# Two layers of SSM convolution and SiLU layer, forward and backward: half of the first layer's activations stored turned, and where the w2 gradient's matmuls are woven in

## The chip, the core and the metric

The kernel runs on one core of a Trainium2 chip. The metric is device microseconds of one execution, lower is better. The core has five engines that are named here as the profile does: PE (TensorE, matmuls; its weight loads are PEld), DVE (VectorE), ACT (ScalarE), POOL (GpSimd) and SP (SyncE, which only issues DMAs here). "SPq" is SP's queue of DMA issues. Each engine works through its own instructions in order and waits on semaphores for the others.

## The reference

Sequence length S = 2048, width D = 448, hidden width F = 1792, batch 1, bfloat16. Four residual blocks are applied to one input, and the kernel returns the output and the gradients with respect to all inputs but `B_x`, for a given `grad_out`:

```python
def _fwd_reference(A_q, A_k, A_v, A_shift_k, A_ssm_k, A_ssm_D, B_x, B_w1, B_w2):
    # _A_ref: k is convolved with a 4-tap kernel and multiplied by v (kv);
    #         y = irfft(rfft(kv, 2S) * rfft(ssm_k, 2S))[:S] + kv * ssm_D;  returns q * y
    # _B_ref: silu(x @ w1) @ w2
    x = A_q
    x = x + _A_ref(_layernorm(x), A_k, A_v, A_shift_k, A_ssm_k, A_ssm_D)
    x = x + _B_ref(_layernorm(x), B_w1, B_w2)
    x = x + _A_ref(_layernorm(x), A_k, A_v, A_shift_k, A_ssm_k, A_ssm_D)
    x = x + _B_ref(_layernorm(x), B_w1, B_w2)
    return x

def reference(...):
    _out, _vjp = jax.vjp(_f, A_q, A_k, A_v, A_shift_k, A_ssm_k, A_ssm_D, B_w1, B_w2)
    return (_out, *_vjp(grad_out))
```

What matters for this case are the gradients of the weights. With a0, a1 the SiLU activations (S x F) of the two dense layers, and g0, g1 the gradients that arrive at those layers' outputs (g1 is `grad_out`), the gradient of w2 is a0ᵀ·g0 + a1ᵀ·g1. The gradient of w1 is built the same way from the layers' normalised inputs and the gradients before the SiLU.

## The kernel before

**Stages.** `_ssm_prefix` computes the convolution y of kv once with a Fourier transform that is written as matmuls; y serves both layers. `Main.run` then goes over the sequence in four chunks of 512 rows, three times: forward of the first dense layer (in the code `L == 0`; the change's short title calls it layer 1), then forward and backward of the second layer (`L == 1`), then backward of the first. `_ssm_suffix` transforms the gradient of y back (a first transform step per index n2, `_fft_stage1`, sixteen of them; transposes; a spectrum and an inverse in seven pieces; two last inverse transforms) and computes the gradients of k, v, the filters and D.

**Activations.** `Main.h` computes half of the hidden width (seven of the fourteen strips of 128) of one chunk: matmuls, SiLU into `aT` on ACT, a copy of the input into `dT` (on DVE, partly ACT) for the slope. Both are feature-major: partition = feature, free = position. `aT` and `dT` have three buffers each. For the first layer `dT` goes to DRAM (`DT_d`, L640) and `aT` too (`store_plain`, L507, `AP_d`); after the first chunk each half also loads one piece of the turned weights (`next_piece`, L516, transposing DMAs). The matmuls of the weight gradients need position on the partitions, so `AP_d` is read back with a transposing DMA. For the second layer `store_turned` (L503/L504) is used: two transposing DMAs from SBUF to SBUF into the single buffer `turned`, and a plain store into `A_d` that is kept back (`self.late`) until the next `flush`; it is read back with a plain DMA.

**Woven matmuls.** The w2 gradient (`_gw2`) goes over fourteen strips `ft`; a strip has two jobs (`_job`), one for each layer: one load of 512 KB into a buffer `dstat` (L896 transposed, L898 plain), then 16 matmuls (L900) with X (g0) or GO (g1) as the moving operand, all 32 into one PSUM tile; then a copy `dout` on ACT and a store. `_gw1` does the same for w1 with `mov` (the normalised inputs, loaded from DRAM: N_d3 at L1032 and N_d1 at L922) and `GH_d`, `GP_d`; there each strip's `dout` also gets a memset on POOL (L959) and a transposing DMA (L936). In all there are 28 strips, 896 matmuls. They are generators: `fill(n)` and `weave(n)` take the next n matmuls and put them at this place of PE's order, with whatever loads and stores they bring. `fill` is used in the backward of the first layer: in `ga` (the product with w2ᵀ, seven PSUM tiles per chunk, 1 each and 2 for the first; none in the first chunk) and in `gn` (the product with w1ᵀ and the sums of the layer norm's backward in `ln_bwd`, four tiles of 128 rows per chunk, 2 each). `weave` is used in the suffix, where `_in_turn` holds PE to the order of the program: 4 after each of the sixteen first transform steps, 16 around each of the transposes, 2 to 5 in the spectrum and the inverse, 3 and 10 in the next stage, 4 and then 34 for each of the eight last transform steps, and at the end all that are left.

**Order.** The order on the engines is the program's, as a scheduler places it when the kernel is built; `issue_after` and `keep_in_program_order` are constraints on it. All loads and nearly all stores stand in SP's one queue.

**The end.** The gradient of k (`grad_k`, eight pieces of two positions each, multiplications and additions on DVE and a store at L1123) is computed for pieces 0 to 5 inside the last transform loop and for 6 and 7 after the last `weave`. Its buffers `gkv` are shared with `gsk`, the gradient of the shift kernel, whose two stores are issued by POOL (L1181, L1182).

Of the kernel before, what the change touches and what calls it, by code (L numbers as in the profile page):

```python
# [11 lines left out]
BF16 = mybir.dt.bfloat16  # L12
# [5 lines left out]
P = 128  # L18
S = 2048
# [3 lines left out]
NT = 16  # L23
DC = 112
ND = 4
NF = 14
# [93 lines left out]
@with_exitstack  # L120
def kernel(
    ctx: ExitStack,
    tc: tile.TileContext,
    A_q: bass.AP,
    A_k: bass.AP,
    A_v: bass.AP,
    A_shift_k: bass.AP,
    A_ssm_k: bass.AP,
    A_ssm_D: bass.AP,
    B_x: bass.AP,  # L130
    B_w1: bass.AP,
    B_w2: bass.AP,
    grad_out: bass.AP,
    out_0: bass.AP,
    out_1: bass.AP,
    out_2: bass.AP,
    out_3: bass.AP,
    out_4: bass.AP,
    out_5: bass.AP,
    out_6: bass.AP,  # L140
    out_7: bass.AP,
    out_8: bass.AP,
):
    nc = tc.nc
    k = K()
    k.tc, k.nc = tc, nc
    k.bal = _Bal(nc)
    for nm, v in (("A_q", A_q), ("A_k", A_k), ("A_v", A_v), ("A_shift_k", A_shift_k), ("A_ssm_k", A_ssm_k),
                  ("A_ssm_D", A_ssm_D), ("B_w1", B_w1), ("B_w2", B_w2), ("grad_out", grad_out)):
        setattr(k, nm, v)  # L150
    k.outs = [out_0, out_1, out_2, out_3, out_4, out_5, out_6, out_7, out_8]
    C = make_fft_consts()

    dram = ctx.enter_context(tc.tile_pool(name="dram", bufs=1, space=DRAM))
    k.KS_d = dram.tile([S, D], BF16, name="KS_d")
    k.SPEC_d = {nm: dram.tile([128, SPEC], BF16, name=f"spec_{nm}") for nm in ("K", "KV")}
    k.N_d = [dram.tile([S, D], BF16, name=f"N_d{i}") for i in range(4)]
    k.DT_d = dram.tile([4, 2, P, NF // 2, 512], BF16, name="DT_d")
    k.A_d = dram.tile([P, NF, NT, P], BF16, name="A_d")
    k.AP_d = dram.tile([NF, P, S], BF16, name="AP_d")  # L160
    k.GH_d = dram.tile([P, NF, NT, P], BF16, name="GH_d")
    k.GP_d = dram.tile([NF, P, S], BF16, name="GP_d")

    bf = mybir.dt.np(BF16)
    m1b = np.ascontiguousarray(C["M1"], dtype=np.float32).astype(bf)
    minv = (np.transpose(m1b.astype(np.float32), (3, 1, 2, 0)) * np.float32(C["inv_scale"])).astype(bf)
    k.m1_h = nc.inline_tensor(np.ascontiguousarray(m1b.reshape(P, -1)), name="c_m1")
    gs_h = nc.inline_tensor(np.ascontiguousarray(C["Gs"].reshape(P, -1)).astype(np.float32).astype(bf), name="c_gs")
    k.minv_h = nc.inline_tensor(np.ascontiguousarray(minv.reshape(P, -1)), name="c_minv")

    keep = ctx.enter_context(tc.tile_pool(name="keep", bufs=1))
    k.ident = keep.tile([P, P], BF16, name="ident")
    make_identity(nc, k.ident[:])
    k.gs_h = gs_h
    k.rstd = [keep.tile([P, J], FP32, name=f"rstd{i}") for i in range(4)]
    k.warm = keep.tile([P, 4], FP32, name="warm")
    k.mhalf = keep.tile([P, 4], FP32, name="mhalf")
    nc.gpsimd.memset(k.mhalf[:], -0.5)
    nc.scalar.activation(k.warm[:], k.mhalf[:], ACT.Silu)
    k.wk = ctx.enter_context(tc.tile_pool(name="wk", bufs=1))  # L180
    k.dp = ctx.enter_context(tc.tile_pool(name="dp", bufs=1))
    k.yk = ctx.enter_context(tc.tile_pool(name="yk", bufs=1, side="right", reuse_waits="tile"))
    k.Ysb = k.yk.tile([P, J, D], BF16, name="Ysb", tag="Y")
    _ssm_prefix(k)
    k.w1sb = k.wk.tile([P, ND, F], BF16, name="w1sb", tag="WA")
    nc.sync.dma_start(out=k.w1sb[:, 0:3, :], in_=k.B_w1[0:384].rearrange("(c p) f -> p c f", p=P))
    nc.sync.dma_start(out=k.w1sb[:, 3, :], in_=k.B_w1[320:448])
    k.w2sb = k.wk.tile([P, NF, D], BF16, name="w2sb", tag="WB")
    nc.sync.dma_start(out=k.w2sb[:], in_=k.B_w2.rearrange("(c p) d -> p c d", p=P))
    k.psum = ctx.enter_context(tc.tile_pool(name="psum", bufs=1, space=PSUM, reuse_waits="tile"))  # L190
    k.xg = ctx.enter_context(tc.tile_pool(name="xg", bufs=1, side="right", reuse_waits="tile"))
    k.Xp = k.xg.tile([P, NT, 512], BF16, name="X", tag="X")
    k.X = k.Xp[:, :, :D]
    k.gYb = k.xg.tile([P, NT, D], BF16, name="gYb", tag="GY")
    k.bal.reset()
    with ExitStack() as es:
        m = Main(k, es)
        m.run()
    _ssm_suffix(k)


# [51 lines left out]
def _pm(ap2d):  # L253
    return ap2d.rearrange("(p j) d -> p j d", j=J)
# [225 lines left out]
class Main:  # L480
# [136 lines left out]
    def h(self, c, L, nT, half, hold, pre=None):  # L617
        nc, k = self.nc, self.k
        aT = self.td.tile([P, NF // 2, 512], BF16, name="aT", tag="T", bufs=3)
        dT = self.td.tile([P, NF // 2, 512], BF16, name="dT", tag="D", bufs=3)  # L620
        hold.append((aT, dT))
        d0 = pre() if pre else None
        for ft0, n, at in ((0, 2, 1), (2, 2, 0), (4, 2, 1), (6, 1, 1)) if half == 0 else ((7, 1, 1), (8, 2, 1), (10, 2, 0), (12, 2, 1)):
            ps = k.psum.tile([P, 2, 512], FP32, name="ps_h", tag="mm", bufs=2)
            self.contract(ps, self.w1sb, nT, ft0, n, at)
            o = ft0 - 7 * half
            a = aT[:, o:o + n, :]
            tm = dT[:, o:o + n, :]
            last = nc.scalar.activation(a, ps[:, 0:n, :], ACT.Silu)  # L629
            e = nc.scalar if o == 4 or (o, c, L, half) == (0, 0, 0, 0) else nc.vector  # L630
            _copy(nc, e, tm, ps[:, 0:n, :])
            k.bal.add("act", 0.52 * n)
            k.bal.add(*(("act", 0.52 * n) if e is nc.scalar else ("dve", 0.6 * n)))
        if L == 1:
            if half == 1:
                with self.tc.issue_after(last.ins):
                    for _, d in hold:
                        self.slope(d)
        else:
            nc.sync.dma_start(out=k.DT_d[c, half], in_=dT[:])  # L640
            self.store_plain(nc.sync, k.AP_d, aT, c, half)
            if c > 0:
                self.next_piece()
        if L == 1:
            self.store_turned(k.A_d, aT, c, half)
        return d0

    def out(self, c, aT, last):
# [77 lines left out]
    def gn(self, c, L, ghT, nb, gres, na, hook=None):  # L726
        nc, k = self.nc, self.k
# [4 lines left out]
        for tl in range(4):  # L732
# [6 lines left out]
            k.bal.add("act", 0.75)  # L739
            k.pe_engine = mm.ins.engine  # L740
            if L == 0:
                self.fill(2)
            if hook:
                hook(tl, mm.ins, last_u.ins)
            g1 = G[:, tl, :]
# [36 lines left out]
    def run(self):  # L782
        k, nc = self.k, self.nc
# [28 lines left out]
        for c in range(4):  # L812
# [26 lines left out]
            na, nb = na1, nb1  # L839
            if c < 3:  # L840
                gb = gb_next
        k.jobs = _gw2(k, k.dp, range(2), [(k.dp, "dstat", 3)], first=k.go_jobs.ins)
        bb = nc.cur_bb.bb

        def fill(n):
# [58 lines left out]
def _gw2(k, pool, fts, slots, bufs=2, first=None):  # L904
    nc = k.nc
    for ft in fts:
        ps = k.psum.tile([P, 512], FP32, name="ps_d", tag="tr", bufs=2)
        for L, mov in ((0, k.X), (1, k.GO)):
            slot = slots.pop(0)
            slots.append(slot)  # L910
            yield from _job(k, ps, k.A_d if L else k.AP_d, ft, mov, slot, L == 0, L == 1, first, L == 0)
        o = pool.tile([P, D], BF16, name="dout", tag="dout", bufs=bufs)
        nc.scalar.copy(o[:], ps[:, :D])
        nc.sync.dma_start(out=k.outs[8][ft * P:(ft + 1) * P, :], in_=o[:])
# [50 lines left out]
def _ssm_suffix(k):  # L965
    nc, tc, bal = k.nc, k.tc, k.bal
# [6 lines left out]
    with ExitStack() as es:  # L973
# [4 lines left out]
        both = [(k.dp, "dstat", 3), (k.dp, "dstat", 3), (dp2, "dstat", 2), (k.dp, "dstat", 3), (dp2, "dstat", 2)]  # L978

        def jobs():  # L980
            yield from k.jobs
            yield from _gw2(k, k.dp, range(2, NF), both)
            yield from _gw1(k, dp2, both)

        jobs = jobs()

        def weave(n):
            with _in_turn(k):
                for _ in zip(range(n), jobs):
                    pass  # L990
# [4 lines left out]
        Z = sp.tile([P, NDH, P], BF16, name="Zg")  # L995
        ksf = k.yk.tile([P, J, D], BF16, name="ksf", tag="Y")
        B1k = A1[:].rearrange("p a c n s -> p (a c n s)").rearrange("p (q d) -> p q d", d=D)
        for n2 in range(16):
            with _in_turn(k):
                _fft_stage1(k, n2, k.gYb[:, n2, :], A1, psum, nc.scalar if n2 < 12 else None)  # L1000
            weave(4)
# [106 lines left out]
        def grad_k(g):  # L1108
            acc = p2.tile([P, 2, D], FP32, name="gk_acc", tag="gK", bufs=4)
            gk = p2.tile([P, 2, D], BF16, name="gk", tag="gk", bufs=2)  # L1110
            last = None
            for j in range(4):
# [7 lines left out]
                    last = acc  # L1120
                else:
                    last = pj
            nc.sync.dma_start(out=out2_pm[:, 2 * g:2 * g + 2, :], in_=gk[:])  # L1123

        out3_pm = _pm(k.outs[3][0])
        out2_pm = _pm(k.outs[2][0])
# [89 lines left out]
```

## Time and profile before

| | |
|---|---|
| time, median of 3 runs | 748.47 us (746.36 to 749.24) |
| the profiled execution | 746.53 us, its span 744.4 us |
| PE busy | 690.7 us, 93% of the span |
| DVE, ACT, POOL busy | 507.0, 424.3, 61.6 us |
| mean granted TensorE clock | 0.985 |
| DMA moved | 172.77 MB, 232 GB/s over the span |

The span runs from the first to the last instruction of the profiled execution; the time contains some 2 us around it. The stages in it: the prefix to about 95 us, the first layer's forward to about 205, the second layer to about 410 (its last part overlaps the next), the first layer's backward to 516, the suffix to the end.

From the groups of instructions and the DMA issues, for the parts that the change touches:

| what | count | duration |
|---|---|---|
| L900 matmul of a woven job (128x448) | 896 | 352 ns recorded, pipelined |
| L736 matmul of `gn` (128x448) | 448 | 353 ns recorded, pipelined |
| AP_d<-aT, plain store from the forward, 896 KB | 8 | 4.1 us to landing |
| turned<-aT, transposing, SBUF to SBUF | 16 | 4.3 us to landing |
| A_d<-turned, plain store, 896 KB | 8 | 4.0 us to landing |
| out_dram<-gk, 224 KB | 8 | 2.7 us to landing |

Matmuls are pipelined, so a recorded duration is longer than the distance from one to the next.

### The profile page before, as it was taken

The page shows a single profiled execution, that of the slowest core. Times are in us where ns is not written, and L with a number is a line of the kernel's source. Part 1 is how long each engine was busy: PE and PEld are TensorE (multiplying, and loading weights), DVE is VectorE, ACT ScalarE, POOL GpSimd, SP SyncE. Part 2 cuts the span into 40 slices and gives each one's busy share as a digit, 9 for nine tenths or more (in the row PEclk, how much of TensorE's full clock was granted, in tenths as well). Part 3 has the DMA queues.
Part 4 walks back from the last instruction along what each step waited for, and adds up shares of the span by engine and source line. Part 5 has one row for each costly group of instructions (what it writes and reads, how often), then busy time and mean ns, then how long its engine had stood idle before and what let it go on. Part 6 is the DMA issues. An engine that isn't in the chain of part 4 may idle for free.

```text
span 744.4 us, 12143 instructions
## 1 busy us (share of the span) xinstructions
PE 690.7 (93%) x4724; PEld 363.0 (49%) x4753; DVE 507.0 (68%) x1059; ACT 424.3 (57%) x539; POOL 61.6 (8%) x109
## 2 busy tenths in 40 slices
PE   5988789999999998999999999994999999999996
PEld 5766533444344443444443444442556677555553
DVE  4878878787733597895949979786117773498241
ACT  4688767767437578487576577644525766321001
POOL 1144221111100002000000000000000000000000
PEclk9999989999999999999999999997999999999999
DMA  9959948999575878879999986964998997999797
GB/s 306 238 182 274 358 176 289 274 250 247 163 152 143 204 162 206 184 204 203 223 235 275 362 232 184 312 160 120 292 216 216 327 302 276 320 242 262 163 214 137
DMA packets 232869, 172.77 MB, mean 232 GB/s; under 512 B 178890, under 2 KB 215566, under 8 KB 231660
## 3 DMA queue, kind: packets, MB, share of 16 engines
q1 hardware_dynamic: 226446, 149.46, 76.8%
q0 software_dynamic: 5744, 22.19, 8.8%
q8 instruction: 37, 0.61, 0.3%
q10 hardware_dynamic: 622, 0.35, 0.2%
q14 instruction: 20, 0.16, 0.1%
HBM read 62.24 MB, written 63.77 MB: 169 GB/s over the span
## 4 chain that ended last, share of the span: by engine, by line
PE 46%; DVE 27%; ACT 8%; issue 7%; DMA 7%; POOL 2%; another core or an unknown queue 2%; SPq 1%; DVEq 0%; ACTq 0%; POOLq 0%
PE ps_d L900 17%; PE ps_h L537 6%; PE ps_o L654 5%; PE ps_g L537 4%; PE ps_n L736 4%; DVE lb_junk L711 4%; DMA KB<-Z 3%; DVE dT L113 3%; DVE lb_u L722 3%; DVE lb_u L754 2%; DVE X L723 2%; PE ps_v L232 2%; PE ps_v L233 2%; DMA K_sb<-in_A_ssm_k_dram 2%
## 5 line engine op out<-in xcount | busy, mean ns | idle before, releaser
L900 PEld LDWEIGHTS <-dstat 128*128 128x128 bf16 x896 | 85.4, 98 | 80.7 <-issue 4.7
L537 PE MATMUL ps_h<-nT,w1sb 128*128 128x512 bf16 (+1 forms) x432 | 103.2, 388 | 7.7 <-DVE dT L113 5.1
L537 PE MATMUL ps_g<-gT,w2T 128*128 128x512 bf16 (+1 forms) x448 | 96.0, 381 | 3.9 <-ACT ghp L686 3.9
L736 PE MATMUL ps_n<-w1T,ghT 128*128 128x448 bf16 x448 | 90.2, 353 | 2.2 <-DVE ghT L694 2.0
L629 ACT ACTIVATE aT<-ps_h 128x1024 bf16<-128x1024 f32 (+1 forms) x64 | 58.4, 915 | 57.6 <-PE ps_h L537 40.6
L654 PE MATMUL ps_o<-w2sb,aT 128*128 128x448 bf16 x448 | 90.1, 353 | 0.0
L900 PE MATMUL ps_d<-mov,dstat 128*128 128x448 bf16 x448 | 87.7, 352 | 2.4 <-DMA dstat<-GP_d 2.3
L113 DVE CAST dT<-ps_h 128x1024 bf16<-128x1024 f32 (+1 forms) x55 | 58.3, 1063 | 30.1 <-ACT aT L629 30.1
L537 PEld LDWEIGHTS <-w1sb 128*128 128x128 bf16 (+1 forms) x448 | 36.3, 97 | 71.5 <-issue 43.7
L537 PEld LDWEIGHTS <-w2T 128*128 128x128 bf16 (+1 forms) x448 | 35.3, 96 | 62.8 <-issue 30.2
L736 PEld LDWEIGHTS <-ghT 128*128 128x128 bf16 x448 | 42.8, 98 | 44.2 <-DVE ghT L694 4.3
L686 ACT CAST ghp<-ps_g 128x1024 bf16<-128x1024 f32 x56 | 55.3, 1006 | 15.1 <-PE ps_g L537 11.2
L654 PEld LDWEIGHTS <-aT 128*128 128x128 bf16 x448 | 42.4, 98 | 42.5 <-issue 3.9
L900 PE MATMUL ps_d<-X,dstat 128*128 128x448 bf16 x224 | 54.6, 360 | 0.2
L900 PE MATMUL ps_d<-GO,dstat 128*128 128x448 bf16 x224 | 51.7, 353 | 0.2
L960 ACT CAST dout<-ps_d 128x448 bf16<-128x448 f32 x14 | 7.5, 534 | 65.4 <-PE ps_d L900 37.3
L738 ACT ACTIVATE lb_u<-ps_n,rstd 128x448 f32<-128x448 f32 x32 | 20.3, 633 | 40.4 <-DVE X L723 17.7
L233 PEld LDWEIGHTS <-pb 128*128 128x128 bf16 x336 | 32.5, 98 | 9.0 <-DVE pb L452 5.6
L232 PEld LDWEIGHTS <-pa 128*128 128x128 bf16 x336 | 32.8, 98 | 7.2 <-DVE pa L451 4.3
L694 DVE TENSOR_TENSOR ghT<-dT,ghp 128x1024 bf16<-128x1024 bf16 (+1 forms) x32 | 19.7, 619 | 20.4 <-ACT ghp L686 20.3
L614 ACT ACTIVATE dTl<-dTl 128x1024 bf16<-128x1024 bf16 (+1 forms) x32 | 29.8, 944 | 4.8 <-DMA dTl<-DT_d 4.8
L655 DVE TENSOR_TENSOR X<-X,ps_o 128x448 bf16<-128x448 bf16 x32 | 19.7, 615 | 16.3 <-PE ps_o L654 16.2
(187 smaller groups left out, 1089.6 us busy)
## 6 DMA issues: line engine op xcount, KB each, us to landing
DT_d<-dT SPq DMA_DIRECT2D x8, 896.0 KB, 6.3
AP_d<-aT SPq DMA_DIRECT2D x8, 896.0 KB, 4.1
A_d<-turned SPq DMA_DIRECT2D x8, 896.0 KB, 4.0
GH_d<-turned SPq DMA_DIRECT2D x8, 896.0 KB, 4.5
dTl<-DT_d SPq DMA_DIRECT2D x8, 896.0 KB, 7.6
dstat<-A_d SPq DMA_DIRECT2D x14, 512.0 KB, 4.5
GP_d<-ghT SPq DMA_DIRECT2D x8, 896.0 KB, 9.6
dstat<-GH_d SPq DMA_DIRECT2D x14, 512.0 KB, 4.2
```

The source lines that it names most:

```text
L113: eng.tensor_copy(out, in_)
L232: nc.tensor.matmul(o, lhsT=pa[:, i * P:(i + 1) * P], rhs=k.Gsb[:, ga, :], start=True, stop=False)
L233: nc.tensor.matmul(o, lhsT=pb[:, i * P:(i + 1) * P], rhs=k.Gsb[:, gb, :], start=False, stop=True)
L537: self.nc.tensor.matmul(o, lhsT=w[lo:hi, b, f:f + P], rhs=r, start=(seen[u] == 1), stop=(seen[u] == ND))
L614: self.k.last_slope = self.nc.scalar.activation(s, s, ACT.Derivative_silu)
L629: last = nc.scalar.activation(a, ps[:, 0:n, :], ACT.Silu)
L654: nc.tensor.matmul(po[:, :D], lhsT=aT[ft // 7][0][:, ft % 7, tl * P:(tl + 1) * P], rhs=self.w2sb[:, ft, :], start=(ft == 0), stop=(ft == N ...
L686: k.last_gh = nc.scalar.copy(gh[:], ps[:])
L711: nc.vector.scalar_tensor_tensor(out=junk[:], in0=u0, scalar=1.0, in1=n_t, op0=ALU.mult, op1=ALU.mult, accum_out=cp[:, 1:2])
L722: nc.vector.scalar_tensor_tensor(out=u0, in0=n_t, scalar=cc[:, 1:2], in1=u0, op0=ALU.mult, op1=ALU.add)
L736: mm = nc.tensor.matmul(pn[:, :D], lhsT=ghT[ft // 7][:, ft % 7, tl * P:(tl + 1) * P], rhs=self.w1T[:, ft, :], start=(ft == 0), stop=(ft == ...
L900: i = k.nc.tensor.matmul(ps[:, :D], lhsT=st[:, t, :], rhs=mov[:, t, :], start=start and t == 0, stop=stop and t == NT - 1)
```

## The change

Four things are edited. In the forward of the first layer the first half of the hidden width (strips 0 to 6) goes through `store_turned` into its own DRAM tensor, ahead of the store of `dT`; the second half is stored plain as before, ahead of the store of `dT`, and after a `flush` that issues the kept-back store of the turned half. Accordingly strips 0 to 6 of the first layer are read back with plain loads and strips 7 to 13 with transposing ones, as before. In the last chunk of the first layer's backward, `gn` takes 12 woven matmuls per tile in the place of 2, from three strips in the place of two. In front of the suffix's first transform step 16 more are woven in. The last two stores of the gradient of k are issued by POOL in the place of SP.

```diff
-    k.A_d = dram.tile([P, NF, NT, P], BF16, name="A_d")
-    k.AP_d = dram.tile([NF, P, S], BF16, name="AP_d")
+    k.A_d = [dram.tile([P, n, NT, P], BF16, name=f"A_d{n}") for n in (NF // 2, NF)]
+    k.AP_d = dram.tile([NF // 2, P, S], BF16, name="AP_d")
...
         else:
+            if half == 0:
+                self.store_turned(k.A_d[0], aT, c, 0)
+            else:
+                self.flush()
+                self.store_plain(nc.sync, k.AP_d, aT, c, 0)
             nc.sync.dma_start(out=k.DT_d[c, half], in_=dT[:])
-            self.store_plain(nc.sync, k.AP_d, aT, c, half)
             if c > 0:
                 self.next_piece()
         if L == 1:
-            self.store_turned(k.A_d, aT, c, half)
+            self.store_turned(k.A_d[1], aT, c, half)
...
             if L == 0:
-                self.fill(2)
+                self.fill(2 if c < 3 else 12)
...
-        k.jobs = _gw2(k, k.dp, range(2), [(k.dp, "dstat", 3)], first=k.go_jobs.ins)
+        k.jobs = _gw2(k, k.dp, range(3), [(k.dp, "dstat", 3)], first=k.go_jobs.ins)
...
-            yield from _job(k, ps, k.A_d if L else k.AP_d, ft, mov, slot, L == 0, L == 1, first, L == 0)
+            plain = L == 0 and ft >= NF // 2
+            yield from _job(k, ps, k.AP_d if plain else k.A_d[L], ft - plain * (NF // 2), mov, slot, L == 0, L == 1, first, plain)
...
-            yield from _gw2(k, k.dp, range(2, NF), both)
+            yield from _gw2(k, k.dp, range(3, NF), both)
...
         B1k = A1[:].rearrange("p a c n s -> p (a c n s)").rearrange("p (q d) -> p q d", d=D)
+        weave(NT)
         for n2 in range(16):
...
-            nc.sync.dma_start(out=out2_pm[:, 2 * g:2 * g + 2, :], in_=gk[:])
+            (nc.sync if g < 6 else nc.gpsimd).dma_start(out=out2_pm[:, 2 * g:2 * g + 2, :], in_=gk[:])
```

## The prediction

> **What bounds the kernel now.** I read the busy shares first, then the table of busy time by stretch, then the order of time on each engine inside the one stretch that stood out, and last the end of the kernel. TensorE is busy 690.7 of 744.4 us, so it is the bound almost everywhere, and the question is where its 53.7 idle us lie. The table by stretches of 20 us (columns: length, then busy us and count of PE, PEld, DVE, ACT, POOL, then granted clock, DMA share, GB/s) answers it for the second half:
>
> ```profile
> 480.00:500.00 20.00, 20.00 (x99) 8.47 (x98) 17.19 (x47) 11.56 (x17) 0.79 (x3) 1.00 0.64 155
> 500.00:520.00 20.00, 10.08 (x46) 4.79 (x45) 15.06 (x47) 7.41 (x12) 0.54 (x1) 0.77 0.58 132
> 520.00:540.00 20.00, 20.00 (x115) 10.69 (x114) 3.06 (x3) 10.83 (x13) 0.00 (x0) 0.97 0.89 274
> 540.00:560.00 20.00, 20.00 (x141) 11.60 (x140) 1.57 (x2) 5.13 (x5) 0.00 (x0) 1.00 1.05 223
> ```
>
> From 480 us until about 720 us PE is full, but for one hole of 9.9 us, at half clock when it ends. What ends the hole is in the order of time on PE and on ACT:
>
> ```profile
> 506.25 0.92 PE L900 MATMUL ps_d<-GO,dstat 128*128 128x448 bf16 x4
> 517.09 0.91 PE L210 MATMUL ps_s<-gYb,M1s 128*128 128x448 bf16 x2 [9.92 <-ACT A1g L111]
> 517.79 1.70 PE L900 MATMUL ps_d<-X,dstat 128*128 128x448 bf16 x4
> ```
> ```profile
> 515.49 0.76 ACT L716 ACTIVATE lb_v<-na_l,lb_cc 128x448 bf16<-128x448 bf16 x1 [4.26 <-DVE lb_cc L713]
> 516.16 1.69 ACT L111 CAST A1g<-ps_s 128x896 bf16<-128x896 f32 x2
> ```
>
> The suffix's transform has two PSUM buffers. PE fills both by 506 us. Their evictions to A1g stand on ACT behind lb_v of the last tile, which waits for the DVE sums of the last chunk; those run without a gap (about 4.74 us per tile) until 515.1. So PE has no work while DVE finishes. The same groups of four matmuls take 0.92 us before the hole and 1.70 after it.
>
> The end of the kernel, in the order of time of the last 55 us, PE, SP, POOL and DVE:
>
> ```profile
> 712.22 0.15 POOL L959 MEMSET dout<- 128x64 bf16 x1 [8.31 <-DMA do<-dout]
> 712.90 0.63 POOL L1181 DMA_DIRECT2D out_dram<-gsk  x1 [0.53 <-issue]
> 717.49 0.63 DVE L1117 TENSOR_TENSOR gkp<-gks,skb 128x896 bf16<-128x896 bf16 x1 [13.01 <-DMA out_dram<-gsk]
> 727.20 1.09 DVE L1119 TENSOR_TENSOR gk<-gk_acc,gkp 128x896 bf16<-128x896 f32 x1
> 728.32 0.46 SPq L1123 DMA_DIRECT2D out_dram<-gk  x1
> 728.89 0.37 SPq L898 DMA_DIRECT2D dstat<-GH_d  x1
> 729.61 5.00 PE L900 MATMUL ps_d<-mov,dstat 128*128 128x448 bf16 x24 [2.09 <-DMA dstat<-GP_d]
> 732.92 1.25 PEld L900 LDWEIGHTS <-dstat 128*128 128x128 bf16 x8 [0.55 <-DMA dstat<-GH_d]
> ```
>
> The last two stores of gk are in SP's queue ahead of the last loads of dstat. SP waits there for DVE, and PE then waits for the loads. DVE itself starts that work at 717.5, because its buffer is held by gsk, whose store stands on POOL behind a memset.
>
> **What the Trainium skill says.** "TensorE: Matmul & The Clock Gate", section "What's actually happening": a PE idle for a window of about 3.4 us falls to half clock and needs about 3.4 us of work to regain it. The trace agrees: the granted clock is 0.50 from 511 to 520 us, 1.00 from 523. "Advanced Engine Details and Errata", section "X-Bar Transpose (TRN2)": transposing DMAs are about as fast as ordinary ones. The trace agrees only roughly: the transposed dstat<-AP_d takes a median of 5.9 us to land, the plain dstat<-A_d 4.5, and SP's issue of the first a median of 3.1 us against 0.35. "DMA: Bandwidth & Descriptors", section "Issuing engines are not separate DMA queues": another issuing engine saves only sequencer time. That is all that moving two gk stores to POOL can do, and it is what is short at 728 us.
>
> **The change part by part.** One woven matmul costs 0.189 us (16 of them in 3.03 us in the chain of waits).
>
> 1. *More fill.* Up to the transform, the kernel before issues 8 + 16 + 16 + 16 = 56 woven matmuls (2 a tile in the last step of a chunk, 8 in its first). The new one issues 8 + 16 + 16 + 8 + 48 = 96, which are exactly the three w2 strips of 32, and then 16 more ahead of the transform: 112. So 56 x 0.189 = 10.6 us of PE work move to the front of the transform, out of the last stretch (174 matmuls after the last special product before, 118 now).
>
> 2. *Does the hole take them?* The last chunk's sums start on PE at 492.6. A tile is now 14 + 12 matmuls, 2.65 + 2.27 = 4.92 us; four end at 512.3, the 16 at 515.3, two transform steps with 4 woven each (2 x 1.14) at 517.6. DVE's 4.74 us per tile are now slightly shorter than PE's 4.92: ACT gets its fourth tile at 510.05 and DVE starts on it at 510.9 instead of 510.3, so the chain ends 0.6 us later and the first A1g eviction is done at 517.7. The third transform step starts at 517.75 instead of 517.09: the hole is gone, at a price of 0.65 us.
>
> 3. *Clock.* Steps three to six start at 517.09 and 522.68, 5.59 us for three periods of 1.134 at full clock, so 2.2 us were lost to the half clock. They come back. After the transform's start all is 2.2 - 0.65 = 1.5 us earlier.
>
> 4. *Loads for the filled matmuls.* The fourth to sixth loads take three buffers in turn: free at about 466, 492.4 and 501.0, needed at 502, 506.6 and 512.3. With 4.5 us to land, the tightest spare is about 6 us. All three are plain now; the transposed ones blocked SP for 8.15 and 9.80 us at 474 and 495. Cost: nothing; a late load would stall PE one for one, and the next ps_n behind it.
>
> 5. *The forward.* Per chunk two transposes (a pair in the first layer-1 chunks: 3.98 us on SP; DMA share 0.84 and 0.83 over 220 to 226, so 5.0 us of all engines) and one wait of the late store. Four pairs: 20 us of DMA and some 16 us of SP. From 103 to 205 us the DMA share is 0.80 of 102 us, so 20 us are spare: it just fits. SP's issues there sum to 9 to 15 us per chunk of some 25. Only stores and the turning of weights (first needed at 231) are behind them, and the dT and aT buffers come round after three half-chunks, over 20 us. I take 0; bounds -0.5 and +5.
>
> 6. *The suffix.* Seven transposed loads become plain; PE doesn't wait for them today, so 0. But w1's products come 56 matmuls earlier: the first needs N_d3, which before was issued at 607.7 and landed 10.2 us later, at 617.9; in the new order it is needed at about 618.5 on the old clock. The second needs N_d1, free to start when X is last read (about 612) and needed at 624.5. Both are 1792 KB, back to back on one queue. I take 1.0 us of stall, bounds 0 and 4.
>
> 7. *gk on POOL.* The waits of 2.1 and 0.5 us in front of PE's last loads go: -2.6. POOL's memsets of dout may now stand behind a gk store; bound 0 to +3.
>
> Sum for PE's own chain: -10.6 - 1.5 + 1.0 - 2.6 = -13.7, so 730.7. What is late next: gk. If gsk's store goes out behind a memset as today (landing at 717.4), DVE ends at 728.3 and gk's store by POOL takes 0.5 to issue and about 4 to land (224 KB by POOL, KS_d: 4.4): 733. If it goes out with its cast, PE's 730.7 holds. I take 732.5: 11.9 us less. On the median, 748.47 - 11.9 = 736.5 (the profiled execution, 746.53 with its span of 744.4, is 1.9 below that median).
>
> **Rivals.**
> - *Filled, but given back later* (gain 3.7 to 8, about 742.5): N_d3, N_d1 and the first GP_d loads come late in the last inverse steps, where SP's gK stores (3.3 us a pair) and kx loads stand, or DVE's gk and POOL's queue keep the end near 738. For it: DMA share is above 0.9 from 605 to 617 and SP is nearly full after 645. Against: five dstat buffers, and today's loads are just in time with the same queue.
> - *No gain* (748): the chain of sums is stretched by the filled matmuls as much as PE is filled. Against: by point 2 PE per tile exceeds DVE by 0.2 us only.
> - *Slower* (about 755): the forward's SP queue and DMA, which have no spare left after point 5, fall behind; DT_d stores land over 20 us late, dT's three buffers run out, and DVE's casts, then PE, wait in each half-chunk. It decides only if SP loses more than about 10 us per chunk; at some 3 us for six half-chunks, 18 us are lost against 12 gained. Against: SP has at least 10 us per chunk to spare and the new work is near 6.
>
> **How the numbers follow.** A difference under 0.5% (3.7 us) can't be told from no change. Likeliest case 0.62, given back later 0.24, no gain 0.05, slower 0.09. In the first two the time falls by over 0.5% (a little of the second excepted): faster 0.86, same 0.06, slower 0.08. The range: the likeliest alone runs from 732 (gsk early, no stall for N_d) to 739.5; taking in most of the second case, 732 to 743.
>
> **What would show it.** Right: PE busy near 20 in 500 to 520 with clock 1.00; transform steps from about 515 us; no wait for A1g near 10 us; 118 woven matmuls after the product of band; PE not waiting for dstat after gk. Wrong: waits of PE for dstat in the last chunk or for mov after 610; DT_d waits on DVE in the forward; an end set by gk's store or by dout's memset behind it.

## The result and the profile after

| | before | after |
|---|---|---|
| time, median | 748.47 us (746.31 to 754.24, five executions) | 741.5 us (739.42 to 742.48, five executions) |
| ratio to before, 95% interval | | 0.9897, 0.985 to 0.9945 |
| span of the profiled execution | 744.4 us | 740.4 us |
| mean granted TensorE clock | 0.985 | 0.991 |
| PE busy, DMA moved | 690.7 us, 172.77 MB | 691.8 us, 176.44 MB |

The time fell by 7.0 us, where 12.0 were forecast. Measured again, both kernels side by side on one chip, it fell by 4.8 us (742.05 against 746.88, ratio 0.994, 0.9913 to 0.9967). So the gain is some 5 to 7 us, no more than the spread of single executions. The table of busy time by stretches of 20 us, of the kernel after, has both halves of the story (columns as in the same table of before: length, then busy us and count of PE, PEld, DVE, ACT, POOL, then granted clock, DMA share, GB/s):

```profile
500.00:520.00 20.00, 19.05 (x102) 9.75 (x101) 14.65 (x43) 8.91 (x17) 0.54 (x1) 1.00 0.64 202
640.00:660.00 20.00, 19.70 (x105) 9.81 (x103) 17.88 (x27) 6.52 (x9) 0.83 (x3) 1.00 0.81 208
660.00:680.00 20.00, 19.08 (x101) 9.48 (x99) 14.54 (x22) 2.68 (x4) 1.49 (x3) 1.00 1.01 243
680.00:700.00 20.00, 16.88 (x282) 9.00 (x280) 10.51 (x15) 2.40 (x4) 0.65 (x4) 0.91 0.94 210
700.00:720.00 20.00, 16.10 (x83) 7.76 (x82) 4.69 (x21) 1.06 (x2) 1.47 (x4) 1.00 0.73 154
```

The first row is the one where PE was busy 10.08 us at a clock of 0.77 before; it is now nearly full, at full clock. The other four rows, of the kernel before:

```profile
640.00:660.00 20.00, 20.00 (x109) 10.14 (x107) 15.40 (x23) 6.48 (x9) 0.68 (x2) 1.00 1.05 278
660.00:680.00 20.00, 20.00 (x108) 10.28 (x107) 17.14 (x24) 3.77 (x6) 1.63 (x4) 1.00 0.96 254
680.00:700.00 20.00, 20.00 (x308) 11.34 (x307) 11.45 (x30) 2.19 (x4) 0.51 (x3) 1.00 0.91 203
700.00:720.00 20.00, 19.82 (x105) 9.84 (x104) 3.65 (x6) 1.81 (x4) 1.61 (x5) 1.00 0.86 190
```

From 680 to 720 PE was full before and idles 7.0 us after. Over 640 to 720 its busy time went from 79.8 to 71.8 us. Before the transform and at its start some 11 us were won (9.0 us of idle time, and 2.0 us that half clock had cost); about 8 of them are lost again in the last stretch as idle time. What PE waits for there, in the table of waits of the kernel after, from 640 us on (us in total, times, longest):

```profile
PE ps_d L904 <- DMA dstat<-GP_d: 7.5, 6, 2.5
...
PE ps_d L904 <- DMA dstat<-GH_d: 0.7, 1, 0.7
```

Before, the waits for dstat<-GP_d in this stretch were two, 2.3 us together. L904 is the line that was L900. One of the waits costs more than its length:

```profile
683.63 6.55 PE L904 MATMUL ps_d<-mov,dstat 128*128 128x448 bf16 x26 [2.45 <-DMA dstat<-GP_d]
```

The granted clock is 0.50 here from 684 to 686 us, which is the 0.91 in the row of 680 to 700. 26 such matmuls took 5.08 us at 668.43, at full clock, so another 1.5 us are lost. The hole in front of the transform, in the order of time on PE (after):

```profile
508.27 2.43 PE L904 MATMUL ps_d<-GO,dstat 128*128 128x448 bf16 x12
510.54 3.19 PE L904 MATMUL ps_d<-X,dstat 128*128 128x448 bf16 x16
...
516.95 0.54 PE L210 MATMUL ps_s<-gYb,M1s 128*128 128x448 bf16 x2 [0.95 <-ACT A1g L111]
```

12 and then 16 woven matmuls stand where PE had nothing, and of the 9.92 us of idle time 0.95 are left.

### The profile page after: what moved, and what is told of

It is laid out like the page before. It is cut to its first block, busy times and chain, and to the rows that moved or that the text cites. A ratio compares the mean times of both kernels' runs of the same rounds, so it can differ in the third digit from the quotient of the medians.

```text
span 740.4 us, 12177 instructions
## 1 busy us (share of the span) xinstructions
PE 691.8 (93%) x4753; PEld 362.6 (49%) x4753; DVE 507.4 (69%) x1059; ACT 423.9 (57%) x539; POOL 62.7 (8%) x111
## 2 busy tenths in 40 slices
DMA packets 233749, 176.44 MB, mean 238 GB/s; under 512 B 179034, under 2 KB 215454, under 8 KB 232540
## 5 line engine op out<-in xcount | busy, mean ns | idle before, releaser
L904 PEld LDWEIGHTS <-dstat 128*128 128x128 bf16 x896 | 84.9, 98 | 87.8 <-DMA dstat<-GP_d 10.7
L904 PE MATMUL ps_d<-mov,dstat 128*128 128x448 bf16 x448 | 92.0, 357 | 8.3 <-DMA dstat<-GP_d 7.5
L904 PE MATMUL ps_d<-X,dstat 128*128 128x448 bf16 x224 | 52.1, 353 | 0.0
L904 PE MATMUL ps_d<-GO,dstat 128*128 128x448 bf16 x224 | 50.3, 353 | 0.0
```

Of the source, the lines that this page charges most:

```text
L904: i = k.nc.tensor.matmul(ps[:, :D], lhsT=st[:, t, :], rhs=mov[:, t, :], start=start and t == 0, stop=stop and t == NT - 1)
```

## The experiments

The theory after the result (T): the front part of the change does what it was meant to, and the last stretch is late because SP, which issues in order, stands still there. In `_gw1` each strip's turned gradient is stored by SP (L933, L934) after a transposing DMA do<-dout (L941), and the store waits until that has landed; the next load of dstat stands behind it. The rivals: (R1) the forward's extra transposes cost time after all; (R2) the two gk stores, moved to POOL, hold the end; (R3) the bandwidth of the DMA engines, not an order of issue, makes the loads late. T rests on the order of time of SP's queue in the kernel after:

```profile
699.74 2.12 SPq L941 DMA_TRANSPOSE do<-dout  x1
704.56 0.39 SPq L933 DMA_DIRECT2D out_dram<-do  x1
704.99 0.50 SPq L934 DMA_DIRECT2D out_dram<-do  x1
705.96 2.50 SPq L900 DMA_TRANSPOSE dstat<-GP_d  x1
708.57 0.51 SPq L902 DMA_DIRECT2D dstat<-GH_d  x1
709.19 1.23 SPq L941 DMA_TRANSPOSE do<-dout  x1
713.41 0.40 SPq L933 DMA_DIRECT2D out_dram<-do  x1
713.86 0.51 SPq L934 DMA_DIRECT2D out_dram<-do  x1
714.43 2.55 SPq L900 DMA_TRANSPOSE dstat<-GP_d  x1
```

and on PE's order of time beside it:

```profile
710.59 6.23 PE L904 MATMUL ps_d<-mov,dstat 128*128 128x448 bf16 x32 [1.46 <-DMA dstat<-GP_d]
719.25 6.23 PE L904 MATMUL ps_d<-mov,dstat 128*128 128x448 bf16 x32 [2.44 <-DMA dstat<-GP_d]
```

SP issues the transpose until 701.86, then nothing until 704.56; the load issued at 705.96 is the one PE starts on at 710.59, 1.46 us late. From 710.42 to 713.41 the same happens, and the load of 714.43 is 2.44 us late at 719.25.

In each experiment the ratio is to the kernel before, run on the same chip.

**The forward alone.** The kernel before, with the turned half of the first layer's activations and nothing else:

```diff
-    k.A_d = dram.tile([P, NF, NT, P], BF16, name="A_d")
+    k.A_d = [dram.tile([P, n, NT, P], BF16, name=f"A_d{n}") for n in (NF // 2, NF)]
...
+            if half == 0:
+                self.store_turned(k.A_d[0], aT, c, 0)
+            else:
+                self.flush()
+                self.store_plain(nc.sync, k.AP_d, aT, c, 0)
...
```

> The kernel before with the turned half alone: no added fill, no weave ahead of the transform, gk by SP. Theory A (the forward's cover is real, the 20 us of extra DMA fall into spare time): same as before within 0.3%, the 9.9 us hole at A1g still there. Rival (part of the missing 5 us is lost in the forward or by DMA): slower than before by 2 to 5 us, with DVE or PE waits for DT_d or turned between 100 and 205 us.

747.27 us, ratio 0.999 (0.9971 to 1.001). The row of the table by stretches over the forward, 103 to 205 us, of the kernel before and of this one:

```profile
103.00:205.00 102.00, 95.81 (x485) 40.24 (x492) 77.59 (x163) 64.35 (x81) 15.23 (x18) 0.97 0.80 226
103.00:205.00 102.00, 95.98 (x497) 41.10 (x502) 77.63 (x161) 66.05 (x83) 15.23 (x18) 1.00 1.04 270
```

The DMA share went from 0.80 to 1.04 and PE's busy time didn't move. R1 is out: by the interval the turned half costs 0.1% at most. It can't be told from no change as a gain either, by itself: in the trace of the kernel before PE waits for no dstat<-AP_d, so plain loads in the place of transposed ones save SP's time where nothing waited for it.

**The fill alone.** The kernel before with the fill of 12, three strips, and 16 matmuls ahead of the transform; nothing turned, gk's stores on SP:

```diff
-                self.fill(2)
+                self.fill(2 if c < 3 else 12)
...
+        weave(NT)
         for n2 in range(16):
```

> The kernel before with the added fill and the weave ahead of the transform alone: activations all stored plain, gk by SP. Theory A (the gain is the filled hole, and what is missing of it is lost in the last stretch in SP's queue): 740 to 745 us, the hole gone, PE waits for dstat<-GP_d of 8 us or more after 650 us. If the turned half matters for the fill, PE waits for dstat<-AP_d stand in 490 to 520 us and the time is nearer to the kernel before.

743.64 us, ratio 0.9943 (0.992 to 0.9966). The wait for A1g is 0.9 us, as in the kernel after, and PE waits 8.6 us for dstat<-GP_d, 2.3 in the kernel before. So the fill alone brings both the gain in front and the loss at the end.

**gk's stores back on SP.** The kernel after, with L1129 as it was:

```diff
-            (nc.sync if g < 6 else nc.gpsimd).dma_start(out=out2_pm[:, 2 * g:2 * g + 2, :], in_=gk[:])
+            nc.sync.dma_start(out=out2_pm[:, 2 * g:2 * g + 2, :], in_=gk[:])
```

> The changed kernel with all gk stores on SP again. Theory A (SP's order limits the end): 1 to 4 us slower than the changed kernel, PE waits again for the last loads behind a gk store. Rival (the last gk stores are beside the point): equal to the changed kernel within 1 us.

742.4 us, ratio 0.9922 (0.9901 to 0.9943); PE waits 8.1 us for dstat<-GP_d. The kernel after has 0.9897 (0.985 to 0.9945) and 0.994 (0.9913 to 0.9967). So moving two gk stores to POOL neither costs nor brings anything that these runs can tell. R2 is out.

**The turned gradient's stores on POOL.** The kernel after, with one edit in `_gw1`, so that SP stands at no store there; PE's order is the same:

```diff
-            nc.sync.dma_start(out=out7w[:, :, ft * P:(ft + 1) * P], in_=o7[:, 0:3, :])
-            nc.sync.dma_start(out=k.outs[7][384:448, ft * P:(ft + 1) * P], in_=o7[0:64, 3, :])
+            nc.gpsimd.dma_start(out=out7w[:, :, ft * P:(ft + 1) * P], in_=o7[:, 0:3, :])
+            nc.gpsimd.dma_start(out=k.outs[7][384:448, ft * P:(ft + 1) * P], in_=o7[0:64, 3, :])
```

> The changed kernel with the two stores of each turned w1 strip issued by POOL in the place of SP; bytes and DMA engines are the same. Theory A (SP waits at these stores for the landing of the transpose, with the next loads of dstat behind them): the PE waits for dstat after 650 us fall from about 8 us to under 3, time 732 to 736. Rival B (the loads are slow because the DMA engines are full): the waits stay, 740 to 743. Rival C (POOL's queue becomes the end: memsets of dout behind stores): waits of ACT for POOL grow, 742 or more.

730.95 us, ratio 0.9763 (0.9727 to 0.9799), and on another chip 732.37 us, 0.9798 (0.9769 to 0.9826): as theory A has it, or slightly better. No wait of PE for dstat is left. SP's queue in this kernel:

```profile
695.35 2.17 SPq L941 DMA_TRANSPOSE do<-dout  x1
697.62 2.88 SPq L900 DMA_TRANSPOSE dstat<-GP_d  x1
700.62 0.50 SPq L902 DMA_DIRECT2D dstat<-GH_d  x1
701.72 1.20 SPq L941 DMA_TRANSPOSE do<-dout  x1
703.01 2.78 SPq L900 DMA_TRANSPOSE dstat<-GP_d  x1
```

The load now follows the transpose at once, and POOL does the standing:

```profile
701.22 0.79 POOL L933 DMA_DIRECT2D out_dram<-do  x1 [4.26 <-DMA do<-dout]
702.00 0.54 POOL L934 DMA_DIRECT2D out_dram<-do  x1
```

Its row of the table by stretches:

```profile
680.00:700.00 20.00, 19.48 (x305) 10.96 (x303) 5.96 (x21) 1.60 (x3) 4.66 (x10) 1.00 1.14 247
```

The bytes of the whole kernel are the same, and in this row the engines move 247 GB/s, where they moved 210 in the same row of the kernel after. R3 is out: the engines had room, and the loads were late because they were issued late. Rival C shows only in that SP's transposes wait 4.5 us, in four places, for POOL's memset of `dout`; ACT waits for POOL nowhere in this stretch, and PE isn't held by it.

**The same edit on the kernel before.** The two lines of the last diff, applied to the kernel before (L928, L929).

> The kernel before with the stores of the turned w1 strips on POOL. Theory A (before the change SP still had loads in hand at the end, so its waits cost only the 2.6 us in front of the last loads): 744 to 748 us; the hole at A1g stays. Rival (SP's stores cost the kernel before as much as the changed one, some 10 us): 736 to 740.

742.68 us, ratio 0.9941 (0.9922 to 0.9961), and the hole of 9.9 us at A1g stays. This lies between what the theory and its rival forecast: the kernel before paid some 4.4 us for this order too, and the kernel after pays about 10. Both of PE's waits for dstat<-GP_d are gone, 2.3 us in the trace of before; where the rest of the 4.4 stands is not shown. They are gone although gk's stores are SP's here as before, and SP stands 7.8 us at them waiting for DVE. With this kernel as the measure (0.9941, and 0.9763 and 0.9798 with the change) the change without the standing SP is worth 1.4 to 1.8%, 11 to 13 us.

**The stores kept on SP, but later.** To tell the standing apart from the mere time that 24 issues take, the kernel after with the stores still issued by SP, held back until the next transposed load has been issued. It has three buffers for the turned gradient in the place of two, and a small warm-up tile shares another's memory to make room:

```diff
-    def store():
+    def store(keep=0):
...
-            store()
-            o7 = pool.tile([P, ND, P], BF16, name="do7", tag="do7", bufs=2)
+            o7 = pool.tile([P, ND, P], BF16, name="do7", tag="do7", bufs=3)
...
+                if L == 0 and n == 1:
+                    with k.tc.issue_after(k.job_load):
+                        store(2)
```

> The changed kernel with the stores of the turned strips still on SP, as many as before, but each held back until the next transposed load of dstat is issued (three buffers of do7). Theory A1 (what hurts is that SP waits at the store for the transpose's landing with a load behind it): near the kernel with the stores on POOL, 731 to 735. Rival A2 (what hurts is SP's issue time, about 1 us a strip): 739 to 743, as the changed kernel.

734.26 us, ratio 0.9832 (0.9807 to 0.9856). SP's queue in the last stretch, from the three traces, with T for the transpose do<-dout, P for a transposed load of dstat, s for the pair of stores, all else left out:

```
before   T P s T P s T P s T P s T s P T P s T s P T P s T P s T P s T P s T s
after    T s P T s P T P s T P s T P s T P s T s P T s P T s P T P s T P s T s
later    T P s T P s T P s T P s T P s T P s T P s T P s T P s T P s T P s T s
```

The store is ahead of the next load after 2 strips of 11 before, after 5 in the kernel after, after none here. SP's waits at these stores in the last stretch, for the kernel after first,

```profile
SPq L933 <- DMA do<-dout: 15.9, 7, 5.5
```

for the kernel before,

```profile
SPq L928 <- DMA do<-dout: 5.9, 7, 1.7
```

and for the kernel with the later stores:

```profile
SPq L933 <- DMA do<-dout: 3.3, 6, 1.5
```

SP stood 15.9 us at these stores, 5.9 before, 3.3 here, and PE's wait for dstat<-GP_d went from 7.5 to 2.6 us. The order by itself is worth 7.8 us (742.05 to 734.26, side by side on one chip). That the third buffer did it is unlikely: in the kernel after no transpose waits for one of its two, and the kernel with the stores on POOL has two. What POOL brings beyond this, 0.3 to 0.7% by the two ratios, is not taken apart: here PE still waits 2.6 us for dstat, with half clock after the longer wait (26 matmuls in 6.78 us at 680.38), and SP still spends the time for issuing.

**Without the turned half.** The kernel with the stores on POOL, less the turned half (the forward and the loads are those of before):

```diff
-                self.store_turned(k.A_d[0], aT, c, 0)
...
+            self.store_plain(nc.sync, k.AP_d, aT, c, half)
```

> The changed kernel with the stores of the turned strips on POOL, and without the turned half: all first-layer activations stored plain and read back transposed. Theory A (the turned half moves 20 us of DMA to the forward and frees nothing that PE waits for): within 1.5 us of the kernel with both, 730 to 733. Rival (the seven plain loads save waits in the fill or the suffix): 734 or more, with PE waits for dstat<-AP_d.

Beside it on the same chip, the kernel after once more (742.05 us, as told above; PE waits 7.4 us for dstat<-GP_d):

> The changed kernel once more, unchanged, beside the others on the same chip: 740 to 743 us, PE waits for dstat<-GP_d near 8 us after 650 us.

And a second time on another chip, beside the kernel with the turned half:

> The same without the turned half, once more. If the turned half is worth nothing: within 1.5 us of the one with it. If it is worth what the two calls seemed to show: 2 to 3 us more, with PE idle longer around 390 to 410 us, where the first dstat loads and the loads of dT stand in one SP queue.

733.6 us, 0.9818 (0.9793 to 0.9844), and again 734.18, 0.9824 (0.9794 to 0.9853). With the turned half it was 0.9763 and 0.9798. Both pairs have the same sign, but the intervals of both overlap, and only the second pair ran on one chip together (732.37 against 734.18). The wait of PE for ghp near 400 us, which the last expectation looks for, goes with the execution and not with the kernel: 2.3 and 0.5 us without the turned half, 0.5 and 1.8 with it. Two more comparisons are in the runs above: the forward alone (747.27 against 747.93), and the fill alone against the kernel after with gk's stores on SP (743.64 against 742.4), which differ by the turned half and nothing else. In all four the kernel with the turned half is the faster, by 0.7 to 2.6 us, and in none do the intervals part. So what the turned half is worth stays open: between nothing and a few us.

**Nine a tile.** The kernel with the stores on POOL, with 9 woven matmuls per tile in the last chunk, which makes PE's tile shorter than DVE's again, and 17 more ahead of the transform:

```diff
-                self.fill(2 if c < 3 else 12)
+                self.fill(2 if c < 3 else 9)
...
-        weave(NT)
+        weave(NT + 17)
```

> The changed kernel with the stores of the turned strips on POOL, 9 woven matmuls per tile in the last chunk in the place of 12, and 33 ahead of the transform in the place of 16 (five more in all). Theory (12 a tile make PE's tile 4.92 us, longer than DVE's 4.74, which holds the sums up by over 1 us): the last lb_v comes 1 us or more sooner after the chunk's first sum, the 0.9 us wait for A1g goes, time 1 to 2 us under the kernel with 12. Rival (the order of ACT alone, not PE's length, holds the sums up): same time within 0.5 us.

The kernel with 12 a tile, run again beside it:

> The changed kernel with the stores of the turned strips on POOL, once more, beside the next: 729 to 732 us.

732.06 us, 0.9777 (0.9748 to 0.9806), beside 732.37 for 12 a tile on the same chip. A tile's sums begin with lb_u, which ACT makes of PE's result, and end with lb_v, which ACT makes once DVE's sums are there. In the trace, the time from the first lb_u to the last lb_v of the last chunk is 19.96 us (491.68 to 511.64), against 21.62 with 12 a tile (493.86 to 515.48) and 20.01 before (495.48 to 515.49), and PE has no wait for A1g. So the chain of sums is shorter by 1.66 us, as the theory has it; the time is the same within 0.5 us, as the rival has it. The one wait of PE that could go was the 0.94 us for A1g, which is less than the interval shows. The rival isn't refuted: with 9 a tile ACT's order came out differently too (see point 2 below), so this run doesn't part PE's length from ACT's order.

The fastest versions are these two: 2.0 to 2.4% under the kernel before. The pair that ran together can't be told apart.

## Why the prediction was right, and where it was not

The direction and the mechanism in front of the transform were right; what the change would find at the end of the kernel was not. The forecast was 5.0 us too low. The 741.5 lies within the range only because the range was widened to take in the rival "given back later" (about 742.5), to which it is nearer than to the likeliest case; nearly all of the miss is one term.

1. *More fill: right.* PE has 112 woven matmuls ahead of the transform and 118 after the product of band, the suffix's last large matmul that is not woven (6 + 32 + 32 + 24 + 24 in PE's order of time), as counted.
2. *The hole takes them: right, at a price that was mis-sized.* Predicted 0.65 us, measured about 1.6: the chain of sums took 21.6 us in the kernel after (493.71 to 515.35), in the place of 20.0. The working compared PE's 4.92 us per tile with DVE's 4.74 and charged the sum of the differences. It left out the order on ACT, here for the first two tiles, in the kernel before and then in the kernel after:

```profile
498.61 0.63 ACT L738 ACTIVATE lb_u<-ps_n,rstd 128x448 f32<-128x448 f32 x1 [2.41 <-DVE G L723]
500.98 0.76 ACT L716 ACTIVATE lb_v<-na_l,lb_cc 128x448 bf16<-128x448 bf16 x1 [1.65 <-issue]
```
```profile
499.22 0.76 ACT L720 ACTIVATE lb_v<-na_l,lb_cc 128x448 bf16<-128x448 bf16 x1 [4.78 <-issue]
499.89 0.62 ACT L742 ACTIVATE lb_u<-ps_n,rstd 128x448 f32<-128x448 f32 x1
```

   Before, ACT did lb_u of the second tile ahead of lb_v of the first; in the kernel after it is placed the other way round for these two tiles, so the second lb_u waited until the first tile's sums were done, and DVE, which needs both, had gaps of 0.9 and 0.2 us. From the first lb_v to the second it is 6.16 us (499.22 to 505.38), where it was 4.75 (500.98 to 505.73): 1.4 of the 1.6 us. The later tiles take 4.99 and 4.98 us, close to PE's 4.92. With 14 + 9 matmuls a tile (4.35 us by 0.189 us each) the 1.66 us came back, but there lb_u of the second tile (496.03) is again ahead of lb_v of the first (497.18). That ACT's order and not PE's longer tile is the main part is read from these times; no run changed one without the other.
3. *Clock: right.* 1.00 in the row of 500 to 520, and the transform's steps follow each other by 1.13 us from the third on (516.95, 518.08, 519.21), where before the first two of them took 2.19 and 2.10 (517.09, 519.28, 521.38, 522.52). The prediction's 5.59 us for three are 5.43 by these starts, and the loss 2.0 us in the place of 2.2. The Trainium skill, "TensorE: Matmul & The Clock Gate", section "What's actually happening", fits here: the 0.95 us that are left of the hole don't lower the clock. In the last stretch the measurement differs from it, and the measurement decides: the page gives an idle window of about 3.4 us, but in a wait of 2.45 us, before 683.63, the granted clock fell to half, and in one of 2.44 us, before 719.25, it did not. So a wait shorter than 3.4 us can't be counted as free of this, and the prediction's sum had no term for it.
4. *Loads for the filled matmuls cost nothing: right.* No wait for dstat in the last chunk.
5. *The forward costs nothing: right*, by the forward alone (0.999). Its reason, that the DMA "just fits", wasn't needed: the share went to 1.04, and PE's busy time stayed.
6. *The suffix, 1.0 us for the loads of N_d: 0.* PE has no wait between 595 and 640 us.
7. *gk on POOL, −2.6 us: this step failed.* It took PE's waits for dstat in the last stretch to be the two in front of the last loads, made by gk's stores ahead of those loads, and expected none to be left. In the kernel after the waits in this stretch grew to 8.2 us (7.5 + 0.7), only 0.3 us of it in front of the last 48 matmuls, where the two waits of before stand; putting gk's stores back on SP changed nothing that can be measured; and the kernel before loses its own two waits when only the stores of do leave SP. The sign of the cause was there to see in the kernel before, where SP stood 5.9 us at the stores of do; the prediction uses SP's queue only where gk's stores stand in it.

The sum again, with the measured terms: PE's own chain of 13.7 us, less 8.2 for the waits that stayed, less 1.0 for point 2, plus 1.0 for point 6, less 1.5 for the half clock at 683.63, makes 4.0 us. Measured were 7.0 and 4.8 us by the medians of the two comparisons, and 4.0 between the two profiled executions: not exact, but the wait for dstat is the only term large enough for the miss. So the rival "given back later" named what took the rest, in part: it had SP nearly full after 645 as its evidence, but looked for the loss at N_d, the first loads of GP_d and the end of DVE's gk. gk was no part of it. Its stores go out at 729.86 and 733.84, before PE's last matmuls at 735.99.

Why the kernel after stands more than the one before: in the order that resulted, five stores, not two, come ahead of the next load; this was tested (the stores kept on SP, but later). The traces show what it did to the lead, the loads that SP has issued beyond the job PE is at: 2.8 jobs at 641 us in both kernels, then 3.9 before and 1.9 after at 660. Why the order came out so when the jobs stand 56 matmuls earlier is not shown.

The prediction leaned on the Trainium skill, "DMA: Bandwidth & Descriptors", section "Issuing engines are not separate DMA queues", for the view that another issuing engine saves only the sequencer's time, "usually small". For gk's stores that held: moving two brought nothing that can be measured. For the stores that wait for a DMA it did not: moving 24 of them, which SP mostly issues in 0.4 and 0.5 us, brought about 10 us. Most of that (7.8 us) came back with the stores still on SP, behind the next load, so it was the standing of what is queued behind them, and not the time to issue. Here the measurement decides.

## What to carry to other kernels

A store that waits for a transfer holds up the queue it stands in: look for waits of the issuing queue itself, not only for waits of the engine that is the bound, and put such a store behind the next load or on a queue with nothing behind it. Work that is moved forward to fill a hole can also change the order in which later loads are queued; check what stands ahead of them before counting the hole as won. When two engines take turns in a chain, look at the order of the third engine between them as well as at their periods: here a swap of two instructions on ACT goes with 1.4 us of the chain. And when several edits are made together, run them apart: here the added fill, with the matmuls ahead of the transform, carries both the gain and the loss, and the turned half and gk's stores, each by itself, can't be told from no change.

## What the runs showed of the hardware

The mean busy share of the DMA engines went to 1.04 in the forward and to 1.14 where the loads were issued earlier, so a share near 1 was no ceiling here. The granted clock fell to 0.50 after an idle time of 2.45 us of PE and not after one of 2.44 (683.63 and 719.25 in the kernel after); at 0.50, 26 woven matmuls took 6.55 us in the place of 5.08. A transpose do<-dout of 128x512 took 4.2 us from its issue to the point at which the store of its result could go (709.19 to 713.41), of which SP's own issue was 1.23 us. POOL needed 0.79 and 0.54 us for the two stores that SP issues in 0.39 and 0.50; PE waited for none of it, SP's transposes 4.5 us for POOL's memsets. The point at which a stage begins moves between executions of one kernel: the last chunk's sums start on PE at 490.28 and 491.01 us in two of the kernel with the stores on POOL.
